# First batch's v rounded in its transfer by GpSimd's queue, the global block last in the first values, w_in issued in two jobs a piece, and a new order of all work

## The chip, the cores and the metric

One core of a Trainium2 chip runs the whole program. The metric is device time in microseconds of that core, the median over several executions. One core has five engines with instruction streams of their own: TensorE (PE in the profile; its weight loads are PEld), VectorE (DVE), ScalarE (ACT), GpSimd (POOL) and SyncE (SP). DMAs are issued from the streams of SP, ACT and GpSimd; all of them are carried out by the same 16 DMA engines.

## The reference

Longformer-like attention over 8 batches, 8 heads, 576 positions of 64 numbers, followed by a two-layer network with softplus between its layers. What is computed:

```
scores = q @ k.T / 8                                       # per batch and head
mask   = |i - j| <= 32, or i global, or j global           # 8 global positions, given as input
attn   = softmax(where(mask, scores, -1e9))
x      = (attn @ v) as 4608 tokens x 512
h      = x @ w_in                                          # 512 x 2048
g      = max(h, 0) + log1p(exp(-|h|))                      # softplus
out    = g @ w_out                                         # 2048 x 512, float32
```

q, k, v, w_in and w_out come as float32 from DRAM; the kernel multiplies in bf16 and accumulates in float32.

## The kernel before

**Blocks.** A batch has 18 blocks of 32 positions. Four blocks make a "pair" n (36 in all), four pairs a tile m of 512 tokens (9 tiles). For one pair, `sc` (L1054) makes the scores of each block against the block before, itself, the block after and the gathered global keys. Then come the maximum `mx`, the exponential `ex` (ScalarE), the sum or its reciprocal `su`, the normalising `no` (GpSimd or VectorE) and a 32x32 transposition `tp` (VectorE). Pairs 0 to 3 are handled in two half-pairs (y = 0 and 1), with the mask added by TensorE itself (`mk`, or within `sc`).

**Global rows.** Queries at global positions see all keys. `add_global` (L948) gives them their own little softmax: scores `sg`, maximum `mxg`, exponential `gexp`, transposition `tpg`, sums of values `ov`, and `gv`, which leaves `vg`, the values that the eight global positions put out and that the values step takes up.

**Values.** `add_values` (L1191) multiplies the normalised weights with v, block by block, into four PSUM banks `xo`, and `xev` copies the banks to `xT`, the transposed tokens. Tile 0 is done in three parts of 128, 256 and 128 tokens (`PIECED`, L357), so that the network can begin early. For each run of blocks the first step of the list (`key` None) is that of the global block, which reads `vg` and opens the accumulation; then come the blocks of keys, which read `vb`.

**Network.** `first` (L1265) makes one chunk of 128 hidden units of h out of `xT` and one quarter of `w_in` (chunks 0 to 3 from piece 0, and so on: the weights come in four pieces of 512 columns, kd 0 and 1 by one DMA, kd 2 and 3 by two). `soft` (L1273) is the softplus on ScalarE, `second` (L1278) the product with `w_out`, `oev` and `store` bring the result out.

**Transfers.** SyncE's queue loads q, k (batches 0 and 1 in six parts each, `load_part`, L512; the order in a batch is `FIRST`) and v (`load_v`, L467: eight DMAs, one for a group of 32 partitions and half the heads, each of 32 x 18 runs of 64 float32) into the float32 tiles `stage`. Engines then round them to bf16 (`cast`, into `qb`, `kb`, `vb`). GpSimd's queue loads `w_in` (`weights_in`, L1331) and `w_out` (`weights_out`) and rounds them on the way. Three holds keep transfers apart: `held` (L1352), a GpSimd copy of one element that waits for the last large q part of batch 0, stands ahead of w_in; `follow` (L753), a tiny DMA on SyncE's queue that reads the end of a weight tile, keeps batch 1's q and k behind w_in's second piece, and batch 1's v behind the first piece of w_out; `landed` (L1416) keeps w_out behind a part of batch 1's k.

**Order.** Each piece of work is a job with its costs and dependencies. `ORDER` (L359) is a written-out list of all jobs: an entry divided by 5 is the job's number in the order of the `add` calls, and the remainder the engine (PE, ACT, DVE, POOL, DMA). So the order within each engine and queue can be read from the list. The jobs' costs in the code are the planner's guesses; the list overrides their choice. Where the planner expects TensorE to be idle in the first 34 us it fills in multiplications of zeros (`warm`, L729).

In the list of before, the queue of GpSimd runs: setup of the mask (`make_near`, `make_neg`, `make_nearer`, `make_keys`), three rounded parts of q and k, `held`, w_in pieces 0 and 1, the two halves of v rounded (`cast` of batch 0, w = 2), w_in piece 2, the normalising of half-pairs 0.1 and 1.0, w_in piece 3, half-pairs 1.1 and 2.1, `make_ends`, `landed`. On SyncE's queue batch 0 comes as q's small part, q part 0, k's three parts, q part 1, v. VectorE makes `gv` of batch 0 behind four maxima of later half-pairs.

## Time and profile before

| | |
|---|---|
| median of three runs | 336.28 us (335.39 to 338.06) |
| the profiled execution, its own time | 334.41 us |
| its span, first to last instruction | 332.7 us |
| TensorE busy | 318.4 us (96%) |
| VectorE, ScalarE, GpSimd busy | 223.6, 225.5, 194.9 us |
| mean granted TensorE clock | 0.995 |

Times in the profile are microseconds from the span's start. In a view in order of time each row has start, length, engine, line, operation, tiles as out<-in, and in brackets how long the engine was idle before and what released it. In a view of groups a row has the count, then the total busy time and the mean of one in ns, then the idle time before. The view of stretches gives, for each stretch, its length, then for PE, PEld, DVE, ACT and POOL the busy time with the number of instructions, then the granted clock, the DMA engines' share and GB/s. A DMA's row stands for its issue; the data arrive later.

### The profile page before, as it was taken

The page shows a single profiled execution, that of the slowest core. Times are in us where ns is not written, and L with a number is a line of the kernel's source. Part 1 is how long each engine was busy: PE and PEld are TensorE (multiplying, and loading weights), DVE is VectorE, ACT ScalarE, POOL GpSimd, SP SyncE. Part 2 cuts the span into 40 slices and gives each one's busy share as a digit, 9 for nine tenths or more (in the row PEclk, how much of TensorE's full clock was granted, in tenths as well). Part 3 has the DMA queues.
Part 4 walks back from the last instruction along what each step waited for, and adds up shares of the span by engine and source line. Part 5 has one row for each costly group of instructions (what it writes and reads, how often), then busy time and mean ns, then how long its engine had stood idle before and what let it go on. Part 6 is the DMA issues. An engine that isn't in the chain of part 4 may idle for free.

```text
span 332.7 us, 12083 instructions
## 1 busy us (share of the span) xinstructions
PE 318.4 (96%) x5279; PEld 170.7 (51%) x5279; DVE 223.6 (67%) x394; ACT 225.5 (68%) x443; POOL 194.9 (59%) x177
## 2 busy tenths in 40 slices
PE   8767799999999999999999999999999999999996
PEld 3536686566555445544454445444544454454453
DVE  6668479977998988897783587839669990440000
ACT  3896577997787669279948963698458547935532
POOL 6496419956795379649979744696274755240000
PEclk9997999999999999999999999999999999999999
DMA  5999999989998999977995996018011011011002
GB/s 155 231 187 205 215 196 163 158 137 237 159 176 135 198 170 168 165 164 154 175 190 137 171 182 111 33 37 205 3 53 46 33 46 77 9 44 53 33 28 98
DMA packets 168860, 42.73 MB, mean 128 GB/s; under 512 B 153320, under 2 KB 165864, under 8 KB 168808
## 3 DMA queue, kind: packets, MB, share of 16 engines
q1 hardware_dynamic: 160664, 28.33, 48.7%
q0 software_dynamic: 6272, 10.49, 13.8%
q10 hardware_dynamic: 1872, 3.15, 2.5%
q8 instruction: 41, 0.67, 0.8%
q14 instruction: 11, 0.09, 0.1%
HBM read 36.71 MB, written 9.44 MB: 139 GB/s over the span
## 4 chain that ended last, share of the span: by engine, by line
PE 88%; DMA 4%; SPq 4%; POOL 2%; issue 1%; ACT 0%
PE o L1281 38%; PE h L1270 37%; PE xo L1235 4%; PE s L1068 3%; DMA win<-in_moe_w_in_dram 3%; SPq L469 2%; DMA stage<-in_v_dram 2%; PE ov L988 2%; PE pick L877 1%; SPq L518 1%; SPq L514 1%; PE sg L959 1%; POOL pn L1123 1%; PE tr L848 1%; POOL win L1335 1%
## 5 line engine op out<-in xcount | busy, mean ns | idle before, releaser
L1270 PE MATMUL h<-xT,win 128*128 128x512 bf16 (+3 forms) x768 | 137.3, 328 | 2.2 <-DMA win<-in_moe_w_in_dram 1.7
L1281 PE MATMUL o<-wout,g 128*128 128x512 bf16 (+1 forms) x592 | 137.0, 374 | 0.0
L1276 ACT ACTIVATE g<-h 128x512 bf16<-128x512 f32 (+3 forms) x192 | 83.9, 499 | 43.4 <-PE h L1270 42.0
L1270 PEld LDWEIGHTS <-win 128*128 128x128 bf16 x768 | 67.5, 99 | 61.2 <-issue 2.7
L1123 POOL TENSOR_TENSOR pn<-st,rs 128x1024 bf16<-128x1024 f32 (+1 forms) x36 | 64.8, 1809 | 40.4 <-DVE rs L1117 28.9
L1281 PEld LDWEIGHTS <-g 128*128 128x128 bf16 x592 | 55.6, 98 | 61.1 <-issue 0.5
L1091 POOL TENSOR_TENSOR st<-st,m 128x1024 f32<-128x1024 f32 x32 | 60.4, 1897 | 30.1 <-DVE m L1085 30.0
L1115 DVE TENSOR_REDUCE sm<-st 128x8 f32<-128x1024 f32 x32 | 38.5, 1203 | 17.2 <-ACT st L1108 17.0
L1072 DVE TENSOR_TENSOR st<-s,mask 128x512 f32<-128x512 f32 x64 | 41.1, 675 | 9.2 <-PE s L1068 9.2
L1085 DVE TENSOR_REDUCE m<-st 128x8 f32<-128x1024 f32 x32 | 38.2, 1205 | 0.4
L1108 ACT ACTIVATE st<-st 128x1024 f32<-128x1024 f32 x32 | 33.0, 1053 | 0.6 <-POOL st L1091 0.5
L1132 DVE STREAM_TRANSPOSE pt<-pn 128x512 int32<-128x512 int32 x36 | 24.6, 690 | 7.8 <-POOL pn L1123 7.6
L720 ACT COPY osb<-o 128x512 f32<-128x512 f32 (+1 forms) x25 | 14.2, 570 | 19.2 <-PE o L1281 17.7
L720 ACT CAST xT<-xo 128x512 bf16<-128x512 f32 (+3 forms) x25 | 11.0, 490 | 16.6 <-PE xo L1235 15.8
L720 DVE CAST xT<-xo 128x512 bf16<-128x512 f32 (+3 forms) x23 | 11.6, 543 | 11.9 <-PE xo L1235 11.9
L1276 ACT ACT_TABLE_LOAD x13 | 16.7, 1283 | 2.6 <-PE h L1270 2.0
L720 POOL CAST vb<-stage 128x1152 bf16<-128x1152 f32 x13 | 15.0, 1167 | 3.9 <-DMA stage<-in_v_dram 3.9
L717 POOL TENSOR_SCALAR qb<-stage 128x1152 bf16<-128x1152 f32 (+2 forms) x12 | 13.3, 1115 | 6.8 <-DMA stage<-in_q_dram 6.8
L1293 POOL DMA_DIRECT2D out_dram<-osb x24 | 13.7, 573 | 5.5 <-DVE osb L720 5.5
L1068 PE MATMUL s<-kx,qx 64*32 64x128 bf16 x1152 | 14.7, 220 | 2.0 <-DVE qx L720 1.5
L1068 PEld LDWEIGHTS <-qx 64*32 64x32 bf16 x1152 | 10.3, 90 | 10.8 <-issue 7.6
L1108 ACT ACT_TABLE_LOAD x12 | 15.4, 1283 | 0.2
(125 smaller groups left out, 293.3 us busy)
## 6 DMA issues: line engine op xcount, KB each, us to landing
stage<-in_v_dram SPq DMA_DIRECT2D x64, 144.0 KB, 4.3
stage<-in_k_dram SPq DMA_DIRECT2D x48, 144.0 KB, 4.1
stage<-in_q_dram SPq DMA_DIRECT2D x48, 144.0 KB, 3.8
out_dram<-osb POOLq DMA_DIRECT2D x24, 256.0 KB, 3.0
out_dram<-osb ACTq DMA_DIRECT2D x11, 256.0 KB, 2.0
stage<-in_q_dram SPq DMA_DIRECT2D x4, 512.0 KB, 7.9
stage<-in_k_dram SPq DMA_DIRECT2D x4, 512.0 KB, 6.9
wout<-in_moe_w_out_dram POOLq DMA_DIRECT2D x4, 512.0 KB, 8.1
```

Source lines behind the costliest of these rows:

```text
L720: {"ACT": nc.scalar.copy, "DVE": V.tensor_copy, "POOL": nc.gpsimd.tensor_copy}[e](out, in_)
L1068: nc.tensor.matmul(out=PS["s", n, g][quad(a), x, :], lhsT=qx[b % 2][rows(g), a, j * BL:(j + 1) * BL], rhs=kx[b % 2][rows(g), a, e0 * BL:(e ...
L1072: V.tensor_tensor(out=PS["st", n][:, h, :, :], in0=PS["s", n, h][:, :, :], in1=mask[:, h, j0:j0 + PB, :, :].rearrange("p j s i -> p j (s i ...
L1085: V.reduce_max(out=m[:], in_=flat(PS["st", n], h0, h1), axis=AX)
L1091: on(e).tensor_tensor(out=t, in0=t, in1=over(PS["m", n, y][:], SL * BL), op=OP.subtract)
L1108: nc.scalar.activation(out=t, in_=t, func=AF.Exp)
L1115: V.reduce_sum(out=sm[:], in_=flat(PS["st", n], h0, h1), axis=AX)
L1123: on(e).tensor_tensor(out=PS["pn", n][:, :, :, h0:h1].rearrange("p x s h -> p h x s"), in0=PS["st", n][:, h0:h1], in1=PS["rs", n, y][:].re ...
L1132: V.transpose(out=bass.AP(base.tensor, base.offset, ap=[list(base.ap[0]), [2 * STEP, PB // 2], [STEP + BL // 2, 2], [1, SL * BL]]), in_=PS ...
L1270: nc.tensor.matmul(out=h[:, :], lhsT=w_in_t[c // 4][:, kd, c % 4 * P:(c % 4 + 1) * P], rhs=PS["xT", m][:, kd, lo:hi], start=(kd == 0), sto ...
L1276: nc.scalar.activation(out=PS["g", m, c][:, lo:hi], in_=PS[key][:, lo_of(c, hi - lo)], func=AF.Softplus)
L1281: nc.tensor.matmul(out=PS["o", m, ns, a][:, :], lhsT=PS["g", m, kf][:, ns * P:(ns + 1) * P], rhs=w_out_t[kf // 4][:, kf % 4, a:z], start=( ...
```

## The change

1. v of batch 0 is no longer loaded by SyncE into `stage` and rounded by GpSimd. GpSimd's queue loads it in four jobs of two DMAs each straight into `vb[0]`, rounding on the way; there is no `cast` for it.
2. `weights_in` is split in two jobs a piece (the DMA of kd 0 and 1; the two of kd 2 and 3), which the order may place apart.
3. Batch 1's q and k wait for w_in's third piece instead of its second (`follow(0, w_in_t[2])`).
4. In the first values (tile 0, first 128 tokens) the global block's step goes from first to last, as a piece of its own that waits for `gv`. As the accumulation must now be opened otherwise, four multiplications by zeros of 128 columns open the four banks.
5. `make_near` and `make_nearer` may run on VectorE; the planner's start of transfers goes from 3050 to 3450.
6. `ORDER` is new throughout. At the start the queue of GpSimd now runs: `make_neg`, one half of q part 0 rounded, the four v jobs, `held`, w_in 0 (both jobs), 1 (both), 2 first job, `make_ends`, 2 second job, 3 first job, half-pair 1.0 normalised, 3 second job, half-pairs 2.0, 2.1, 3.1, a rounded part of batch 1's q, `blank`, another, `landed`. SyncE's has q part 0, k's three parts, q part 1, q's small part, and then batch 1. VectorE takes `make_near`, `make_nearer`, `make_keys` and half-pairs 0.0, 0.1, 1.1 and 3.0. ScalarE runs: four slots of the mask, eight rounded parts of batch 0's q and k with four copies of k between them, then `ex` 0.0, 0.1, a copy of q, `ex` 1.1, a small copy, `ex` 1.0, `gexp` twice, `ex` 2.0, 2.1, `gv`, `ex` 3.1, three copies to `xT`, `ex` 3.0, the first softplus. TensorE has twelve chunks of `first` for the first 128 tokens ahead of the second values (eleven before), four behind them, and then the next 256 tokens' chunks, with batch 1's transpositions behind the first of these (two groups of four stood ahead of them before).

```diff
     def load_v(eng, b, h, rs):
         for c in rs:
-            eng.dma_start(out=stage[2][quad(c), h, :, :],
+            eng.dma_start(out=stage[2][quad(c), h, :, :] if b else vb[0][quad(c), :, h * D:(h + 1) * D],
                           in_=SRC[2][b, HG * h + c].rearrange("(m i) d -> i m d", i=BL))
...
-        if w == 2:
+        if w == 2 and not b:
+            last = None
+            T["cast", 0, 2] = []
+            for h in range(2):
+                for x in range(2):
+                    last = T["half", 0, h] = o.add({"POOL": (1300, 0)}, lambda e, h=h, x=x: load_v(nc.gpsimd, 0, h, range(2 * x, 2 * x + 2)), [last], rank=0,
+                                                   moves=1400, late=1600 if h else 300)
+                    T["cast", 0, 2].append(last)
+            T["load", 0, 2] = last
+        elif w == 2:
...
-                    follow(0, w_in_t[1])
+                    follow(0, w_in_t[2])
...
+        ahead = v_ == 0
+        if ahead:
+            steps = steps[1:] + steps[:1]
...
                 for r in range(KD):
                     PS["xo", v_, r] = psum(("xo", v_, r), [P, 512], FP32)
+                    if ahead:
+                        nc.tensor.matmul(out=PS["xo", v_, r][:, 0:cols], lhsT=idle[:, 0, :], rhs=idle[:, 0, 0:cols], start=True, stop=False)
...
-            ready += [T["gv", b]] + T["cast", b, 2]
+            ready += ([] if ahead else [T["gv", b]]) + T["cast", b, 2]
...
-    def weights_in(x):
+    def weights_in(x, y):
         cols = moe_w_in[:, x * WC:(x + 1) * WC]
-        nc.gpsimd.dma_start(out=w_in_t[x][:, 0:KD // 2, :], in_=cols[0:HD // 2].rearrange("(a p) f -> p a f", p=P))
+        if not y:
+            nc.gpsimd.dma_start(out=w_in_t[x][:, 0:KD // 2, :], in_=cols[0:HD // 2].rearrange("(a p) f -> p a f", p=P))
+            return
...
     for x in range(4):
-        last = T["w_in", x] = o.add({"POOL": (1400, 0)}, lambda e, x=x: weights_in(x), [last or T["held"]],
-                                    rank=-1 if x else 0, hold=2000 if x else 0, moves=2950)
+        for y in range(2):
+            last = T["w_in", x] = o.add({"POOL": (1300 if y else 650, 0)}, lambda e, x=x, y=y: weights_in(x, y), [last or T["held"]],
+                                        rank=-1 if x else 0, hold=2000 if x else 0, moves=1475)
...
-    add_cast(0, 2)
```

More of the change, by code (lines that the diff above doesn't have):

```diff
@@ L106 @@
     DEEP, QUANTUM, RING = 8500, 500, 2600
-    BEGIN = 3050
+    BEGIN = 3450
     PACKETS = {1: 1024, 2: 256, 4: 576, 8: 1152}
```

17 lines of the change are left out of this document (9 added, 8 removed), and 144 rows, old and new, of the table ORDER.

## The prediction

> **What bounds the kernel now.** I read the page first: which engine is full, and which queues move the data.
>
> ```profile
> PE 318.4 (96%) x5279; PEld 170.7 (51%) x5279; DVE 223.6 (67%) x394; ACT 225.5 (68%) x443; POOL 194.9 (59%) x177
> ...
> q1 hardware_dynamic: 160664, 28.33, 48.7%
> q0 software_dynamic: 6272, 10.49, 13.8%
> ```
>
> TensorE is the bound, and its work is not changed but for four multiplications. So only its 14.3 us of idle time (332.7 - 318.4), its filling with zeros and the time at a lower clock can be won. Next, where that lies: the view of TensorE's waits, over the whole execution and after 47 us.
>
> ```profile
> PE xo L1235 <- DVE vg L1001: 2.1, 1, 2.1
> PE h L1270 <- DMA win<-in_moe_w_in_dram: 1.7, 1, 1.7
> PE ov L988 <- POOL vb L720: 1.7, 1, 1.7
> ```
> ```profile
> PE xo L1235 <- issue: 0.4, 1, 0.4
> ```
>
> After 47 us one wait of 0.4 us is left (and the end, which the change leaves as it is). The case is decided by when TensorE enters the stretch without waits. TensorE in order of time, from the first product with w_in on:
>
> ```profile
> 29.03 3.53 PE L1270 MATMUL h<-xT,win 128*128 128x128 bf16 x44
> 32.49 0.32 PE L1235 MATMUL xo<-pt,vg 32*64 32x256 bf16 x8
> 32.63 0.84 PE L1235 MATMUL xo<-pt,vb 32*64 32x32 bf16 x80
> 33.40 0.40 PE L1270 MATMUL h<-xT,win 128*128 128x128 bf16 x4
> 34.32 0.29 PE L1270 MATMUL h<-xT,win 128*128 128x128 bf16 x2 [0.52 <-ACT g L1276]
> 36.33 0.72 PE L1270 MATMUL h<-xT,win 128*128 128x128 bf16 x10 [1.72 <-DMA win<-in_moe_w_in_dram]
> 36.88 0.81 PE L729 MATMUL warm<-vb 128*128 128x512 bf16 x3
> 37.53 0.39 PE L848 MATMUL tr<-ident,kb 128*128 128x128 bf16 x4
> ...
> 38.41 0.81 PE L1270 MATMUL h<-xT,win 128*128 128x256 bf16 x6
> ```
>
> Eleven chunks of the first 128 tokens, the second values at 32.49, then chunks 11 and 12 and a stop: chunk 12 gets two of its four multiplications at 34.32, the others at 36.33, when the late DMAs of w_in's last piece have landed. At 38.41 the chunks of the next 256 tokens begin, and from there TensorE is fed. This 38.41 is the mark that I move. Why was w_in late? GpSimd's and SyncE's queues, and GpSimd's groups of 12 to 29 us:
>
> ```profile
> 14.82 0.95 POOL L1333 DMA_DIRECT2D win<-in_moe_w_in_dram  x1
> ...
> 20.79 1.34 POOL L720 CAST vb<-stage 128x1152 bf16<-128x1152 f32 x1 [0.72 <-DMA stage<-in_v_dram]
> ...
> 26.75 1.21 POOL L1335 DMA_DIRECT2D win<-in_moe_w_in_dram  x2
> ```
> ```profile
> 7.51 0.60 SPq L514 DMA_DIRECT2D stage<-in_q_dram  x1
> 8.16 7.41 SPq L469 DMA_DIRECT2D stage<-in_v_dram  x8
> 24.88 0.73 SPq L757 DMA_DIRECT2D trail<-win  x1
> ```
> ```profile
> L1335 POOL DMA_DIRECT2D win<-in_moe_w_in_dram x8 | 4.9, 627 | 0.0
> L1123 POOL TENSOR_TENSOR pn<-st,rs 128x512 bf16<-128x512 f32 x4 | 4.2, 1079 | 0.0
> L1333 POOL DMA_DIRECT2D win<-in_moe_w_in_dram x4 | 3.2, 805 | 0.0
> L720 POOL CAST vb<-stage 128x1152 bf16<-128x1152 f32 x2 | 2.6, 1283 | 0.7 <-DMA stage<-in_v_dram 0.7
> ```
>
> GpSimd issues w_in from 14.82 to 27.96 (26.75 + 1.21), and 8.1 us of that (4.9 + 3.2) is issuing; the rest is v's rounding (2.6, and 0.7 of waiting for v) and half-pairs. The transfer rates by stretch (5 to 9 us: q and k; 13 to 18: v; 19 to 24: w_in; 27.5 to 31: w_in's end beside batch 1):
>
> ```profile
> 5.00:9.00 4.00, 4.00 (x14) 1.44 (x12) 1.74 (x6) 1.90 (x5) 3.25 (x9) 1.00 1.18 310
> 13.00:18.00 5.00, 4.86 (x119) 2.53 (x114) 3.88 (x13) 4.42 (x17) 4.52 (x8) 1.00 1.39 186
> 19.00:24.00 5.00, 2.23 (x122) 1.61 (x130) 4.04 (x12) 5.00 (x28) 4.28 (x5) 1.00 1.23 197
> 27.50:31.00 3.50, 3.42 (x69) 2.83 (x70) 2.74 (x4) 3.15 (x16) 3.07 (x4) 0.51 1.03 234
> ```
>
> The DMA engines are full all the while; and in the last stretch the granted clock is 0.51, just after the wait for vg.
>
> **The change, part by part.** *v by GpSimd's queue.* What goes: 7.4 us of SyncE's queue (nothing waits behind it until 24.88, so this alone is worth nothing), 2.6 us of rounding on GpSimd, and the wait of `ov` for it (1.7). What comes: eight issues on GpSimd, each of 32 x 18 = 576 runs. No row has so many; the nearest are 627 ns (128 runs) and 805 ns (256), so 5.0 to 6.4 us, and I take the upper end, because the time grows with the runs. They stand behind one rounded half of q part 0, whose arrival ScalarE saw at 7.10:
>
> ```profile
> 7.10 0.63 ACT L713 ACTIVATE qb<-stage 128x512 bf16<-128x512 f32 x1 [5.01 <-DMA stage<-in_q_dram]
> ...
> 16.18 0.39 ACT L1104 ACTIVATE st<-s,m 128x128 f32<-128x128 f32 x1
> ```
>
> That part is now the first on its queue, so 7.10 + 0.6 is a late bound for v's start. v is issued by 7.7 + 6.4 = 14.1 at the latest, 12.7 at the earliest; and `held` costs no wait, as its part, last of the large ones at 7.51 before, has landed by then.
>
> How long v takes to arrive: 4608 runs. At the mean of the hardware queue's packets (48.7% x 332.7 x 16 / 160664 = 16 ns) that is 4.6 us on 16 engines, at the mean of the software queue's (13.8% x 332.7 x 16 / 6272 = 117 ns) 34 us. The nearest row is the same v in the stretch 13 to 18: 1.18 MB at 186 GB/s, 6.3 us. The 117 ns belongs to packets of 1.7 KB (10.49 MB / 6272). I take 6.3, so v is there at about 16 to 17; TensorE's `ov` needs it after 22. So v has some 5 us of slack. The Trainium skill ("DMA: Bandwidth & Descriptors", Specifications) says that transfers under 512 B make the DMA engine read, modify and write, which speaks against this edit, since rounding halves v's written runs from 256 to 128 B. The rows bear it out as far as they go: 186 GB/s for v's 256 B against 310 for q and k; one more such step (x 0.6) would be an estimate of 10.5 us instead of 6.3, still inside the slack, though w_in behind it on the same queue would come up to 4 us later.
>
> *w_in in two jobs.* It starts at about 13.7 instead of 14.82. To the end of piece 3's first job GpSimd has 8.1 - 1.25 = 6.8 us of issuing and one short copy: 21 us. Then half-pair 1.0 (1.08) stands ahead of the last job and waits for VectorE, which gives its factor after the global transposition: about 24 to 25, as below. So the last job is issued at about 25 to 26.2 (27.96 before). Batch 1's q and k now wait for piece 2 and so start later, at about 27; w_in's last 256 KB find the engines empty. Their data alone are 1.3 us at 197 GB/s, which would be 27.5; the 9.6 us from 26.75 to 36.33 once more would be 35.8. With the engines empty I take 31. Batch 1's parts start 1 to 2 us later, but no longer beside 0.5 MB of w_in; their third is due at 35, its transposition on TensorE after 36: margin 1 us, and that is what is late next.
>
> *The way to the second values.* ScalarE's chain starts at 16.18. ScalarE has now more copies ahead of it, VectorE waits for q part 1 instead of GpSimd, six small mask operations go from GpSimd to VectorE (which is busy 1.74 of 4 us between 5 and 9, so they hide). I take 15.5, between 14.8 (q arrives 1.4 us earlier, all else follows) and 16.9. The groups of ScalarE, 13 to 32 us:
>
> ```profile
> L1104 ACT ACTIVATE st<-s,m 128x128 f32<-128x128 f32 x32 | 11.3, 440 | 1.0 <-DVE m L1083 1.0
> ...
> L971 ACT ACTIVATE pg<-sg,gnb 128x320 bf16<-128x320 f32 (+1 forms) x2 | 1.1, 636 | 0.0
> ```
>
> A half-pair is 11.3 / 8 = 1.41. To the first `xT`: seven half-pairs 9.9, one copy and a small one about 1.0 (an estimate from the 0.63 of the same size at 7.10), the global ones 1.1, `gv` 0.3 (an estimate, half of that 0.63), so 27.8, and the copies 0.6: first product at 28.4 (29.03 before). The global block last hides 40 of 48 multiplications of the first values beside `ov` and `gv`; but `gv` is queued on ScalarE behind six half-pairs, so this gains what the wait of 2.1 was only in part: it is in the 28.4. Twelve chunks are 48 multiplications: 44 took 3.53 us with the clock at half for most of it, so 3.9 for 48 at that pace, 2.9 at the 10 in 0.72 less overlap. That gives 31.3 to 32.3; the second values' other inputs (VectorE's half-pair 1.1 behind `ex` 3.1, and two transpositions) come at 30 to 31.8. I take 31.6 for the mark 32.49: 0.9 us won, with 0.25 us of a chunk more done by then.
>
> *The stop.* From the end of the second values (33.47) to 38.41 are 4.94 us. Of these 1.2 are five chunks (20 multiplications at 60 ns), 0.75 two groups of transpositions that now come later. The rest, 3.0, is the waits of 0.52 and 1.72, 0.65 of zeros (36.88 to 37.53) and small change. With w_in landed at 31 all of it goes.
>
> Sum: -0.9 - 0.25 - 3.0, and +0.2 for four opening multiplications: **-3.9 us** at the mark, kept to the end since no wait lies behind it. Against the profiled execution's own 334.41 (span 332.7 and 1.7 around it) that is 330.5. The median of the runs stands 1.9 above the profiled one; from it, 336.28 - 3.9 = **332.4**.
>
> **Rivals.** *1. v delays q and k; no change that can be measured.* The loads of batch 0 were alone on the DMA engines until v followed them on the same queue. Now v comes from another queue while q part 1 is under way. For it: 27.5 to 31, where w_in and batch 1 share the engines and w_in's last DMA needs until 36.33. Against it: from 5 to 9 alone, at 310 GB/s, 1.2 of q and k's 2.4 MB are through, and v begins at 8 or later. Price: if v takes half the packets, q part 1 comes up to 2 to 3 us later, ScalarE's start goes to 18, the front loses 2 to 2.5 and the stop still gains 3.0: -0.5, 335.8. Half of that delay: 334.5. The Trainium skill ("DMA: Bandwidth & Descriptors", Queues, rings and completion order) has each engine go round its queue rows packet by packet, which is this rival's mechanism; that stretch agrees, but no row has two such streams of small runs.
>
> *2. Small packets of the software queue are dear; slower.* w_in stands behind v on one queue. At 117 ns v would end at 42; at 70 ns its 4608 runs take 20 us and end at 29, the first piece of w_in lands at 32 instead of before 29.03, the third chunk (which needs piece 2) waits to 37, and the mark goes to some 41 to 42: 340. It decides from about 50 ns a packet (14.4 us, v at 23, w_in's last piece at 34 to 36). For it: the only mean of that queue is 117. Against: its packets are seven times larger.
>
> *3. More is won.* If the clock stays up over the first chunks (0.51 in 27.5 to 31: 44 multiplications in 3.53 could be 2.6, and the zeros before them) and ScalarE starts at 14.8, another 1.5 to 2: 330.5.
>
> **How the numbers follow.** Forecast, within 1.5 us of 332.4: 0.45; rival 3: 0.13; rival 1 and its half: 0.25; rival 2: 0.17, of which 0.02 small. The range leaves out rival 2's worse part above 338.5, and the tail of rival 3 below 328.5. Runs of this kernel spread by 0.8%, so about 1% (3.4 us, 332.9) is what tells a change from none. Faster: rival 3 and some three quarters of the forecast, 0.48; within 1%: rival 1, the rest of the forecast and rival 2 where small, 0.37; slower: rival 2, 0.15.
>
> **What would show it.** In the changed profile: v's issues on GpSimd at 7 to 14 and of 0.6 to 0.8 us each; first exponential at 15 to 16; no wait of TensorE for v or w_in; the second values near 31.6 and the 256-token chunks near 33.7. If the exponentials start after 17, rival 1 is on; if TensorE waits for w_in longer than 2 us, rival 2. A new wait of TensorE for a part of batch 1 or for w_out would mean that the gain was given back there.

## The result, and the profile after

The changed kernel takes 333.76 us in the median of 12 runs (332.56 to 338.17) against 336.44 us (335.39 to 342.76) of the kernel before beside it: a ratio of 0.9928, 95% interval 0.9907 to 0.9948. That is 0.7% faster, so "within 1%"; 332.4 had been forecast. The profiled execution takes 333.06 us, span 331.4. Now and then an execution is over 1.5% slower than the fastest of its kernel; the ratios, and the counts of runs by clock under "The median and the profiled run", leave these out.

The page of the changed kernel, the rows that answer to those of before:

```profile
PE 317.9 (96%) x5281; PEld 168.8 (51%) x5281; DVE 220.9 (67%) x387; ACT 231.7 (70%) x460; POOL 193.3 (58%) x173
...
q1 hardware_dynamic: 155928, 27.15, 46.0%
q0 software_dynamic: 11008, 11.08, 17.0%
```

The queue of GpSimd (q0) has 4736 packets more: v's 4608 and 128 others. TensorE is as full as before. Now GpSimd and ScalarE at the start, in order of time (start, length, engine, line, operation, tiles):

```profile
6.20 5.53 POOL L469 DMA_DIRECT2D vb<-in_v_dram  x8
...
12.86 0.73 POOL L1350 DMA_DIRECT2D win<-in_moe_w_in_dram  x1 [0.42 <-DMA vb<-in_v_dram]
...
24.45 1.24 POOL L1353 DMA_DIRECT2D win<-in_moe_w_in_dram  x2
```
```profile
14.96 0.35 ACT L1113 ACTIVATE st<-s,m 128x128 f32<-128x128 f32 x1
```

v is issued from 6.20 to 11.73, w_in from 12.86 to 25.69 (14.82 to 27.96 before), and the exponentials begin at 14.96 (16.18). TensorE, from the global rows' values to the chunks of 256 tokens:

```profile
22.81 1.23 PE L997 MATMUL ov<-vb,pgt 32*32 32x129 bf16 x72 [0.99 <-DVE pgt L987]
...
25.06 0.64 PE L1237 MATMUL xo<-vb 128*128 128x128 bf16 x4
25.69 0.49 PE L1251 MATMUL xo<-pt,vb 32*64 32x64 bf16 x40
25.99 0.29 PE L1251 MATMUL xo<-pt,vg 32*64 32x128 bf16 x8
...
27.63 2.84 PE L1286 MATMUL h<-xT,win 128*128 128x128 bf16 x48 [0.81 <-DMA win<-in_moe_w_in_dram]
30.40 0.32 PE L1251 MATMUL xo<-pt,vg 32*64 32x256 bf16 x8
...
31.38 1.94 PE L1286 MATMUL h<-xT,win 128*128 128x128 bf16 x24
```

The last row joins multiplications that follow without a gap and names the shape of the first: the last 16 for the first 128 tokens, then eight for the next 256. A view from 32.5 us on shows the eight in a row of their own:

```profile
32.28 1.04 PE L1286 MATMUL h<-xT,win 128*128 128x256 bf16 x8
```

The wait for the rounded v and the stop for w_in are gone. The mark, the first chunk of 256 tokens, came from 38.41 to 32.28: 6.1 us. Of these 0.7 are two groups of transpositions that stood ahead of the mark before and now stand behind it (33.15 and 34.79), so TensorE is 5.5 us ahead with the same work. But the last store is issued only 1.8 us earlier (330.07 before, 328.25 after), and the span is 1.3 us shorter. The view of stretches shows where the rest went; here are the kernel before and then the changed one (length, busy time of each engine with its number of instructions, granted clock, transfer share, GB/s):

```profile
38.00:46.00 8.00, 7.69 (x177) 6.79 (x176) 3.87 (x7) 6.57 (x22) 4.88 (x12) 1.00 0.99 159
46.00:54.00 8.00, 7.92 (x212) 7.02 (x212) 6.94 (x12) 3.99 (x15) 4.28 (x4) 1.00 0.96 181
54.00:62.00 8.00, 8.00 (x90) 4.15 (x89) 7.86 (x14) 7.79 (x13) 7.65 (x5) 1.00 1.24 181
62.00:70.00 8.00, 8.00 (x183) 4.58 (x181) 7.74 (x18) 7.41 (x16) 7.66 (x6) 1.00 0.83 131
```
```profile
38.00:46.00 8.00, 7.62 (x222) 5.94 (x220) 6.99 (x11) 6.64 (x22) 2.83 (x4) 1.00 1.11 168
46.00:54.00 8.00, 6.41 (x153) 4.05 (x151) 5.80 (x9) 4.73 (x16) 6.67 (x5) 1.00 1.22 193
54.00:62.00 8.00, 8.00 (x115) 4.16 (x114) 7.16 (x13) 5.02 (x8) 4.69 (x4) 1.00 1.03 167
62.00:70.00 8.00, 6.90 (x182) 4.58 (x180) 5.89 (x11) 7.54 (x17) 7.74 (x6) 1.00 0.90 143
```

TensorE (first busy column) works 31.6 of 32 us in the kernel before and 28.9 in the changed one: of the gain 2.7 us are lost as idle time between 38 and 70 us, 1.5 of them in 46 to 54 and 1.1 in 62 to 70. (The 5.5 us are 1.7 at 69 us, so 3.8 are given back; of the other 1.1 these columns show nothing.) In order of time, the rows of the changed kernel there:

```profile
47.16 0.68 PE L1077 MATMUL s<-kx,qx 64*32 64x128 bf16 x56 [0.58 <-issue]
52.81 0.43 PE L968 MATMUL sg<-kx,qg 128*32 128x320 bf16 x8 [1.00 <-issue]
57.77 1.14 POOL L720 CAST vb<-stage 128x1152 bf16<-128x1152 f32 x1 [3.31 <-DVE sm L1124]
60.80 1.06 ACT L1117 ACTIVATE st<-st 128x1024 f32<-128x1024 f32 x1 [2.96 <-POOL st L1100]
64.67 0.22 PE L1251 MATMUL xo<-pt,vg 32*64 32x64 bf16 x4 [0.40 <-ACT osb L720]
66.60 1.90 POOL L1132 TENSOR_TENSOR pn<-st,rs 128x1024 bf16<-128x1024 f32 x1 [0.26 <-DMA stage<-in_q_dram]
69.31 0.38 PE L1251 MATMUL xo<-pt,vg 32*64 32x384 bf16 x8 [0.23 <-DVE pt L1141]
```

Two things are to be seen. TensorE stands twice with nothing to wait for but its own instructions ("issue", 0.58 and 1.00). And GpSimd stands 3.31 us ahead of a rounding (57.77), which is the second half of batch 1's v; behind it on GpSimd is a subtraction for the softmax, for which ScalarE stands 2.96 us, and because ScalarE is late with its copies out of PSUM, TensorE stands at the values between 63.9 and 65.3 (0.40 us at 64.67, for a copy on ScalarE). The last of four products on GpSimd ends at 68.50, and 0.81 us later, after a transposition on VectorE, TensorE begins the values that need it (32x384, "the fifth values" below).

### The profile page after: what moved, and what is told of

Same layout as the page of the kernel before. It is cut to its first block, busy times and chain, and to the rows that moved or that the text cites. A ratio compares the mean times of both kernels' runs of the same rounds, so it can differ in the third digit from the quotient of the medians.

```text
span 331.4 us, 12080 instructions
## 1 busy us (share of the span) xinstructions
PE 317.9 (96%) x5281; PEld 168.8 (51%) x5281; DVE 220.9 (67%) x387; ACT 231.7 (70%) x460; POOL 193.3 (58%) x173
## 4 chain that ended last, share of the span: by engine, by line
PE 71%; SPq 11%; DMA 9%; ACT 4%; issue 1%; POOL 1%; DVE 1%; POOLq 0%
PE o L1297 32%; PE h L1286 29%; SPq L464 5%; PE xo L1251 4%; DMA stage<-in_q_dram 4%; SPq L469 3%; PE s L1077 3%; DMA stage<-in_k_dram 3%; ACT st L1113 2%; DMA wout<-in_moe_w_out_dram 2%; PE ov L997 1%; DMA stage<-in_v_dram 1%; SPq L518 1%; PE pick L886 1%; SPq L514 1%
## 5 line engine op out<-in xcount | busy, mean ns | idle before, releaser
L1297 PE MATMUL o<-wout,g 128*128 128x512 bf16 (+1 forms) x592 | 138.6, 374 | 0.2 <-ACT g L1292 0.2
L1286 PEld LDWEIGHTS <-win 128*128 128x128 bf16 x768 | 66.7, 98 | 59.7 <-issue 1.1
L720 ACT COPY osb<-o 128x512 f32<-128x512 f32 (+1 forms) x27 | 15.5, 575 | 20.3 <-PE o L1297 18.7
L720 POOL CAST kb<-stage 128x1152 bf16<-128x1152 f32 (+2 forms) x9 | 11.5, 1273 | 10.8 <-DMA stage<-in_q_dram 8.8
L717 POOL TENSOR_SCALAR qb<-stage 128x1152 bf16<-128x1152 f32 (+1 forms) x11 | 12.9, 1177 | 8.1 <-DMA stage<-in_q_dram 6.5
L720 POOL CAST vb<-stage 128x1152 bf16<-128x1152 f32 x9 | 10.3, 1150 | 6.8 <-DVE sm L1124 3.3
```

Source lines behind the costliest of these rows:

```text
L720: {"ACT": nc.scalar.copy, "DVE": V.tensor_copy, "POOL": nc.gpsimd.tensor_copy}[e](out, in_)
L1286: nc.tensor.matmul(out=h[:, :], lhsT=w_in_t[c // 4][:, kd, c % 4 * P:(c % 4 + 1) * P], rhs=PS["xT", m][:, kd, lo:hi], start=(kd == 0), sto ...
L1297: nc.tensor.matmul(out=PS["o", m, ns, a][:, :], lhsT=PS["g", m, kf][:, ns * P:(ns + 1) * P], rhs=w_out_t[kf // 4][:, kf % 4, a:z], start=( ...
```

## The experiments

My first theory was that both kinds of stop had given the gain back and that each could be taken away by itself. The rival was that ScalarE and GpSimd are full behind 50 us and take back any lead. (In `ORDER` the cuts show the entries that move; the lines they stand in are broken anew, and no other entry changes its place.)

**The changed kernel once more,** as the yardstick of the next three.

> The changed kernel itself, as the yardstick for the three kernels that run beside it: both theories expect the ratio measured first, 0.991 to 0.995 of the kernel before.

332.88 us, ratio 0.9918 (0.9884 to 0.9951). Its rows, for the comparisons:

```profile
57.55 1.14 POOL L720 CAST vb<-stage 128x1152 bf16<-128x1152 f32 x1 [2.32 <-DMA stage<-in_v_dram]
66.37 1.90 POOL L1132 TENSOR_TENSOR pn<-st,rs 128x1024 bf16<-128x1024 f32 x1 [0.26 <-DMA stage<-in_q_dram]
69.07 0.38 PE L1251 MATMUL xo<-pt,vg 32*64 32x384 bf16 x8 [0.22 <-DVE pt L1141]
```

Here the rounding's wait is put down to what it reads, the transfer of v. (VectorE's sum, named in the first trace, is no input of it.)

**Batch 1's v rounded behind the subtraction.** Entry 2008 (the rounding on GpSimd) goes behind 1923 (the subtraction of pair 7):

```diff
     ORDER = (
...
-        2008,
...
         1923,
+        2008,
```

> One step moved: GpSimd rounds the second half of batch 1's v behind the fourth subtraction, not ahead of it. In the changed kernel GpSimd stood 3.31 us ahead of that rounding (54.46 to 57.77), ScalarE then 2.96 us for the subtraction behind it (57.84 to 60.80), and TensorE some 1.5 us at 63.5 to 65.3, where the banks of the fourth values were freed late. My theory: what was won ahead of 38 us was given back at single places of the order, this one among them, so the subtraction starts near 54.5, ScalarE's wait falls below 1 us, TensorE's stop at the fourth values falls from about 1.5 us to under 0.4, and the time by 0.8 to 1.5 us against the changed kernel (ratio to the kernel before near 0.989 to 0.990). The rival: from 50 us on ScalarE and GpSimd are full and take back whatever TensorE is ahead, so the stop moves to a later place and the time stays within 0.4 us of the changed kernel.

331.89 us, ratio 0.9866 (0.9816 to 0.9917; the interval overlaps that of the changed kernel beside it). The trace:

```profile
56.99 1.90 POOL L1100 TENSOR_TENSOR st<-st,m 128x1024 f32<-128x1024 f32 x1 [2.05 <-DVE m L1094]
58.83 1.14 POOL L720 CAST vb<-stage 128x1152 bf16<-128x1152 f32 x1
59.94 7.46 POOL L1132 TENSOR_TENSOR pn<-st,rs 128x1024 bf16<-128x1024 f32 x4
...
64.33 0.24 PE L1251 MATMUL xo<-pt,vg 32*64 32x64 bf16 x8
...
68.20 0.38 PE L1251 MATMUL xo<-pt,vg 32*64 32x384 bf16 x8
```

The stop at the fourth values (64.33) is gone, the four products end at 67.40 and the fifth values come at 68.20, 0.87 us earlier than in the kernel beside it; the span is 0.9 us shorter (330.2 for 331.1). That is the lower end of the expected 0.8 to 1.5. ScalarE's wait fell as expected, to 0.60 us, but the subtraction came at 56.99 and not near 54.5, because it now waited 2.05 us for a maximum on VectorE instead.

**TensorE's stops for instructions.** Ten second products are spread ahead of the dense scores (1945, 1855: pairs 8 and 6; 2010: the global block), and two softplus steps on ScalarE (1181, 1176) come forward with them:

```diff
+        1420, 1585, 1590, 1595, 1600, 1181, 1176,
         1945, 1855,
...
+        1620, 1495, 1500, 1505, 1425,
         2010,
```

(The same entries are taken out further on.)

> Five second products are moved ahead of the scores of pairs 8 and 6, and five ahead of the global block's scores of batch 1 (two softplus steps are moved forward on ScalarE to free their bank). In the changed kernel TensorE stood 0.58 us inside the first scores and 1.00 us ahead of the second with nothing to wait for but its instructions, each time until 1.35 us behind the end of a 16-KB transfer of instructions. My theory: these are the instruction fetch, 64 matmuls and as many weight loads in 0.7 us use up what is loaded; with second products there, which use 2 instructions in 0.22 us, both stops shrink to under 0.3 us each and the time falls by 0.5 to 1.5 us against the changed kernel. The rival: the fetches are asked for by the instructions issued, so they come later by as much, and the stops move to the next dense place: time within 0.4 us.

334.98 us, ratio 0.9981 (0.9943 to 1.0018); the profiled run has 332.58 and span 330.9.

```profile
69.03 0.38 PE L1251 MATMUL xo<-pt,vg 32*64 32x384 bf16 x8 [0.23 <-DVE pt L1141]
```

Both stops for instructions are gone from the trace, and nothing came of it: the fifth values start at 69.03 (69.07). So the stops were real, but not on the path; this half of my theory fell. TensorE only arrived earlier at a place where it waits for GpSimd. Why the median lies 2.1 us over the changed kernel's while the trace is as fast, the traces don't show: 6 of its 12 runs were granted a clock of 0.995 or less, but so were 5 of the 12 of the changed kernel beside it. That stays open.

**Both together.**

> Both moves together. My theory: they lie at different places of the same chain of TensorE's work and add, 1.3 to 3.0 us less than the changed kernel, which gives a ratio to the kernel before of 0.984 to 0.989. The rival (a full ScalarE or GpSimd behind 50 us takes it back): no more than 0.5 us less than the changed kernel.

332.94 us, ratio 0.9911 (0.9877 to 0.9946); fifth values at 69.08, span 331.1: no gain, as the rival said. The scores of pair 8 now come later, VectorE and then GpSimd start later by as much, and the rounding comes so late (59.71) that TensorE stands 1.29 us ahead of the product that reads it. What the spread products put off was the start of GpSimd's chain.

**The parts of the change, one by one.** First, the order of the blocks in the first values, undone:

```diff
-        ahead = v_ == 0
+        ahead = False
...
-        at = [p * len(steps) // pieces for p in range(pieces + 1)] if not ahead else [0, len(steps) - 1, len(steps)]
+        at = [p * len(steps) // pieces for p in range(pieces + 1)] if v_ else [0, len(steps) - 1, len(steps)]
```

> The changed kernel with the global block first in the first values again, so that all of them wait for the global values; the opening multiplications by zeros (four, 0.64 us) fall away. My theory: the global values are ready within 0.3 us of the first values' start in the changed kernel (keys' values from 25.69, global ones at 25.99), so this part of the change is worth next to nothing: time within 0.4 us of the changed kernel, either side. The rival: the order of the blocks is worth the 0.5 us and more that the kernel before waited there, 0.5 to 1 us slower than the changed kernel.

334.13 us, ratio 0.9929 (0.9901 to 0.9957), not to be told from the changed kernel.

```profile
25.73 0.47 PE L1251 MATMUL xo<-pt,vg 32*64 32x128 bf16 x8 [0.52 <-ACT vg L1008]
```

The first values wait 0.52 us for the global ones, and the second values come at 30.38, as with the change (30.40). By the times this part is worth nothing here. Its profiled run took 335.65 us: TensorE stood 1.44 and 1.87 us for instructions (until 32.24 and 45.45), at other places than in the changed kernel, from which this one differs by eight instructions ahead of there; and from 46.62 to 50.03 the granted clock was 0.50. So here the fifth values come at 71.61, 2.3 us later than in the changed kernel.

Then the last piece of w_in, its two jobs together again:

```diff
-        98, 103, 425, 296,
+        98, 103, 108, 425, 296,
```

> The changed kernel with the two jobs of the fourth piece of w_in one behind the other on GpSimd, ahead of the product it used to stand between. My theory: the product's inputs come at 23.46 anyway, 2.42 us after the first job's issue, so 1.24 us of issue fit in between, the fourth piece lands about 3 us earlier, and the time is the same within 0.4 us, as the piece wasn't waited for. The rival: the split is where the gain comes from, the product is late and the time 0.5 us or more above the changed kernel.

333.54 us, ratio 0.9927 (0.9897 to 0.9957): the split of this piece is worth nothing either. The trace shows something else:

```profile
49.87 0.68 PE L1077 MATMUL s<-kx,qx 64*32 64x128 bf16 x56 [1.80 <-issue]
...
61.18 0.80 PE L997 MATMUL ov<-vb,pgt 32*32 32x129 bf16 x72
```
```profile
69.31 0.38 PE L1251 MATMUL xo<-pt,vg 32*64 32x384 bf16 x8
```

TensorE is 1.9 us behind the changed kernel at 61.18 (59.24 in the repeat), after 1.80 us of waiting for instructions, and yet the fifth values start only 0.24 us later. Up to there TensorE has that much slack; GpSimd has none.

And the hold on batch 1's parts, back to w_in's second piece:

```diff
-                    follow(0, w_in_t[2])
+                    follow(0, w_in_t[1])
...
-            T["part", b, w, t] = o.add({"DMA": (700 if b else 0, 0)}, emit, had(("w_in", 2)) + T["cast", 0, w] if b else [], rank=0,
+            T["part", b, w, t] = o.add({"DMA": (700 if b else 0, 0)}, emit, had(("w_in", 1)) + T["cast", 0, w] if b else [], rank=0,
```

> The changed kernel with batch 1's parts held only for the second piece of w_in, as before, not for the third: their transfers run beside the last two pieces. My theory: the parts start 2 to 4 us earlier, the copy of batch 1's keys that the scores waited 0.4 us for at 40 us is earlier, and the third and fourth pieces land later; the first products would wait for w_in some 1 us or more, as the transfers share the 16 engines: time 0 to 1 us above the changed kernel. The rival: the hold costs more than it gives, the earlier parts take 0.4 us or more off the time.

333.92 us, ratio 0.9949 (0.9920 to 0.9979).

```profile
31.78 0.27 PE L1286 MATMUL h<-xT,win 128*128 128x128 bf16 x2 [1.59 <-DMA win<-in_moe_w_in_dram]
```

The stop for w_in is back, 1.59 us (1.72 in the kernel before), as expected; the second values come 1.6 us later. So it is the hold that removes that stop. But the fifth values come at 69.22, 0.15 us later, and the time isn't to be told from the changed kernel's. The rival, that earlier parts are worth more, falls.

**GpSimd's chain made earlier.** With these results I formed the theory anew: behind 50 us the path is the maxima on VectorE, the subtractions on GpSimd, the rounding of batch 1's v when it has landed, four products, a transposition, the fifth values. So the step that the subtraction waited for in the run of the later rounding was moved: VectorE takes the maximum of the global block's scores (2017) behind that of pair 7 (1917).

```diff
-        2008,
...
         1923,
+        2008,
...
-        2017,
...
         1917,
+        2017,
```

> The later rounding again (GpSimd rounds the second half of batch 1's v behind the fourth subtraction), and on VectorE the maximum of the global block's scores of batch 1 behind the masks and the maximum of pair 7 instead of ahead of them. With the later rounding alone the subtraction still stood 2.05 us for that maximum (54.95 to 56.99) and the rounding was over at 59.97, too late for the global values' product, which waited. My theory: the maximum then comes near 55, the subtraction starts within 0.4 us of 54.95, the rounding within 0.5 us of v's landing near 57.5; TensorE's wait ahead of the global values' product goes, no stop at the fourth values, the fifth values start 1.5 to 2.5 us earlier than the 69.07 of the changed kernel, and all behind that by as much: time 1.3 to 2.5 us under the changed kernel (ratio 0.983 to 0.988). The rival: GpSimd's products behind it (7.46 us for four) or ScalarE hold the fifth values where they were with the later rounding alone (68.20): at most 1 us under the changed kernel.

332.67 us in 6 runs, ratio 0.9905 (0.9868 to 0.9942); the profiled run 331.6, span 329.9.

```profile
56.30 1.90 POOL L1100 TENSOR_TENSOR st<-st,m 128x1024 f32<-128x1024 f32 x1 [0.61 <-DVE m L1094]
58.14 1.14 POOL L720 CAST vb<-stage 128x1152 bf16<-128x1152 f32 x1
59.25 7.47 POOL L1132 TENSOR_TENSOR pn<-st,rs 128x1024 bf16<-128x1024 f32 x4
...
67.83 0.38 PE L1251 MATMUL xo<-pt,vg 32*64 32x384 bf16 x8
```

The products end at 66.72, 1.55 us earlier than in the changed kernel's repeat, the fifth values start 1.24 us earlier, and the span is 1.2 us shorter (329.9 for 331.1). By the trace the direction held, but the size stayed under the expected 1.3 to 2.5 us: the scores ahead of the chain stood 1.33 us for instructions in this run, and the subtraction before this one came at 51.95, 0.75 us later than with the later rounding alone (51.20). By the times the rival came ("at most 1 us under"): 332.67 against 332.88 us, and the interval of the ratio overlaps that of the changed kernel.

**And with the second products spread.**

> As the kernel before this one, and the ten second products moved ahead of the scores of pairs 8 and 6 and of the global block's scores, so that the instruction fetch is not waited for. My theory: TensorE's two stops of 0.55 and 0.9 us go as well, and since the rounding no longer stands in the way of the products, they are kept: 0.3 to 1 us under the kernel beside it, 2 to 3 us under the changed kernel. The rival: the fifth values are set by GpSimd's chain (subtraction, rounding at v's landing, four products), which TensorE's earlier hand-over does not move: the fifth values start within 0.3 us of the kernel beside it and the times agree within 0.4 us.

331.82 us in 6 runs, ratio 0.9887 (0.9851 to 0.9922); fifth values at 68.10, span 330.2. By the time it is as the theory said, 0.85 us under the kernel before it, though the intervals overlap; by the trace it is as the rival said, with the fifth values 0.27 us later and the span 0.3 longer. The stops for instructions are gone, but the later scores cost GpSimd 0.6 us (products from 59.82), so the theory's way to its number isn't what the trace shows.

Over these ten traces, all with the changed kernel's front or nearly so, the fifth values start 0.80 to 1.11 us after GpSimd's last product ends, wherever that is, and the span ends 261.8 to 262.3 us behind them (last product's end, fifth values, span):

```
changed kernel                 68.50   69.31   331.4
changed kernel, repeat         68.27   69.07   331.1
spread                         68.23   69.03   330.9
spread, later rounding         68.28   69.08   331.1
global block first             70.62   71.61   333.9
w_in's last together           68.32   69.31   331.4
hold on second piece           68.23   69.22   331.5
later rounding                 67.40   68.20   330.2
later rounding, maximum        66.72   67.83   329.9
both, and spread               67.30   68.10   330.2
```

In six of them TensorE stands for the transposition behind the last product and starts 0.05 us after it ends. In the other four (global block first, w_in's last together, the hold, the maximum) it starts 0.24 to 0.36 us after it, so there TensorE itself is the later one, by that little.

**The first part alone.** Batch 0's v by GpSimd's queue in the kernel before, with the old order otherwise: four issues in GpSimd's idle time from 8.6 us, four ahead of w_in.

```diff
     ORDER = (
...
+        34, 183,
         283,
...
+        39, 188,
         63,
...
-            eng.dma_start(out=stage[2][quad(c), h, :, :],
+            eng.dma_start(out=stage[2][quad(c), h, :, :] if b else vb[0][quad(c), :, h * D:(h + 1) * D],
...
+                if w == 2 and not b:
+                    load_v(nc.gpsimd, b, h, range(R))
```

> The kernel before with one part of the change: batch 1's predecessor, batch 0's v, goes by GpSimd's queue straight to its rounded place, four issues in GpSimd's idle time from 8.6 us (before its first rounding) and four ahead of the first job of w_in; its two roundings on GpSimd fall away; the rest of the order is the old one. My theory: v lies there by about 20.5 us, TensorE's stops of 1.68 us for the rounded v at 20.5 and most of the 2.10 us for the global values at 25.5 go, the start of the 256-token chunks comes 1.5 to 2.5 us earlier than 38.41, and 0.5 to 2 us of the time are won (ratio 0.994 to 0.998): part of the gain, since the exponentials still begin where they did. Rival 1 of the prediction: the small packets take transfer time from q and k, so the second q part is rounded over 0.5 us later than 13.47 and the time stays within 0.5 us of the kernel before. Rival 2: dear packets, slower by over 1 us.

338.35 us, ratio 1.0051 (1.0021 to 1.0081): 0.5% slower. But the run doesn't answer the question, since the planner's costs had put 13 multiplications by zeros into TensorE's way at 13.88 and the first scores came 4.5 us late:

```profile
13.88 3.36 PE L729 MATMUL warm<-vb 128*128 128x512 bf16 x13
```

So once more, with the two costs set so that the zeros stand where they stood in the kernel before:

```diff
-                T["half", b, h] = o.add({"DMA": (2200 if b else 0, 0)}, emit, deps, rank=0, units=R, moves=3100 if b else 2800, late=LATE if b else 1300 * h)
+                T["half", b, h] = o.add({"DMA": (2200 if b else 0, 0)}, emit, deps, rank=0, units=R, moves=3100 if b else 0, late=LATE if b else 1300 * h)
...
-                cost = {"POOL": (1150, 1250), "DVE": (760, 850)}
+                cost = {"POOL": (2000, 5000) if w == 2 else (1150, 1250), "DVE": (760, 850)}
```

> The kernel before with batch 0's v alone sent by GpSimd's queue to its rounded place, as the run of that part before, but without the 13 multiplications by zeros that had been put ahead of the 64-token key transposes there and held the first scores to 18.30 (13.83 in the kernel before). Four issues lie in GpSimd's idle time from 8.6 us, four ahead of the first job of w_in, no roundings. My theory: the first scores come within 0.7 us of 13.83, TensorE's stop of 1.68 us for v at 20.5 goes, w_in's first jobs start 2.9 us later (17.7 for 14.8) but its third at 22 as before; 0 to 2 us of the time are won, less than the changed kernel's 2.7, since the old order still starts the exponentials late. The rival: the new place for v is worth nothing without the new order, since what is late next (the queries' rows at 20.09 and the global values at 27.58) was late by as much: within 0.5 us of the kernel before, either side.

338.17 us, ratio 1.0063 (1.0034 to 1.0093). The first scores came at 14.84, 0.3 us beyond the bound expected, with the clock at 0.50 from 12.48 to 15.90, but the front was then ahead: the third values at 42.77 (44.52 before), the global block's scores of batch 1 at 53.17 (55.23). Then:

```profile
61.15 1.15 ACT L720 CAST vb<-stage 128x1152 bf16<-128x1152 f32 x1 [5.77 <-DMA stage<-in_v_dram]
65.99 0.80 PE L988 MATMUL ov<-vb,pgt 32*32 32x129 bf16 x72 [3.81 <-ACT st L1108]
```

Again it is batch 1's v: ScalarE stands 5.77 us for its second half, TensorE 3.81, and the lead of 2 us becomes a lag (fifth values at 74.94, 70.97 before). The clock has a part in that lag: behind the stop it was 0.50 for 3.41 us (67.10 to 70.51), which costs some 1.7 us (an estimate, half of 3.41). In the kernel before the same rounding started at 57.34 without a wait. What had changed for that transfer? It is issued at 45.62 to 50.99 (45.16 to 51.12 before), but the third and fourth pieces of w_out came on GpSimd's queue at 49.24, 2.3 us earlier than before (51.57), since the subtraction ahead of them came at 47.39 instead of 49.72. So the last run moves the fourth piece of w_out behind the rounding and one subtraction:

```diff
-        823, 1969, 1978, 1808,
+        1969, 1978, 1808, 823,
```

> As the kernel before with batch 0's v alone sent by GpSimd's queue, and the fourth piece of w_out issued behind GpSimd's rounding of batch 1's v and one subtraction (near 54.5 us) instead of ahead of both (50.1). In the run without this edit the early part was ahead of the kernel before by 1.75 us at the third values (42.77 for 44.52) and by 2.06 us at the global block's scores of batch 1 (53.17 for 55.23); then ScalarE stood 5.77 us for the second half of batch 1's v (61.15), TensorE 3.81 us, and the end was 2.2 us later than in the kernel before. My theory: v of batch 1, on SP's queue, shared the transfer engines there with 512 KB that came 2.3 us earlier than in the kernel before; without them ScalarE's rounding starts 1.5 to 3 us before 61.15, TensorE's stop falls to 1 to 2.3 us, the fifth values come 1.5 to 2.6 us before 74.94, and the time is 1.5 to 2.6 us under that run's. The rival: the landing is set by the queue that v stands in, the packets ahead of it and their rate, not by what GpSimd's queue moves: landing within 0.7 us of 61.15 and the time within 0.5 us of that run's.

335.78 us, ratio 1.0008 (0.9973 to 1.0043).

```profile
59.28 1.16 ACT L720 CAST vb<-stage 128x1152 bf16<-128x1152 f32 x1 [3.20 <-DMA stage<-in_v_dram]
64.13 0.80 PE L988 MATMUL ov<-vb,pgt 32*32 32x129 bf16 x72 [1.33 <-ACT st L1108]
```

The landing comes 1.87 us earlier and TensorE's stop falls to 1.33, though the front was 0.7 to 1 us later this time (third values at 43.75, after a clock of 0.50 from 11.72 to 18.55); the fifth values come at 72.37, 2.57 us earlier, and the time falls by 2.4 us: the theory's numbers. The rival, a landing within 0.7 us, falls. 512 KB on GpSimd's queue had held back v on SyncE's. Not all of the 2.4 us is the landing's, as behind this shorter stop the clock doesn't fall to half. And with this mended the first part is still only equal to the kernel before. The Trainium skill ("DMA: Bandwidth & Descriptors", Queues, rings and completion order) has each transfer engine go round the queues that have work; these two runs agree, with 1.87 us as the price here.

## Why the prediction was right, and where it was wrong

333.76 us lies in the range of 328.5 to 338.5, 1.4 us over the forecast. The mechanism was right up to the mark, the size there was too small, and the way from the mark to the end was wrong. Step by step:

- *v by GpSimd's queue.* Start at 6.20 ("7.10 + 0.6 is a late bound"), eight issues in 5.53 us (bounds 5.0 to 6.4, the upper end taken): 0.69 each. In the trace's packet records v's 4608 packets run from 10.5 to 16.1 us, 5.7 us (6.3 taken, there "at about 16 to 17"). That 6.3 was a quotient of bytes and rate; v's 256-byte packets in the kernel before ran from 12.1 to 20.0, 8.0 us. The Trainium skill's rule on transfers under 512 B ("DMA: Bandwidth & Descriptors", Specifications), worked out in the prediction to an estimate of 10.5 us, is not borne out as a further slow-down here: the 128-byte runs took 5.7 us against 8.0 for the 256-byte ones, with a packet at 32 ns against 28 in the median. No engine's computing waited for batch 0's v; GpSimd's issues of w_in stood 0.42 and 0.41 us (12.86 and 15.39), which the trace puts down to v's transfer.
- *w_in in two jobs.* Last issue at 25.69 (25 to 26.2). TensorE's one wait put down to w_in is the 0.81 ahead of the first product. ScalarE's copies to `xT` end at 27.58 and the product starts at 27.63, so it is hardly w_in; in the run with the global block first the same place reads 0.57 for ScalarE's copies. Whether two jobs a piece were needed is another matter: for the last piece they weren't; it is the hold on the third piece that took the stop of 1.72 away.
- *The way to the second values.* Exponentials at 14.96 (15.5), first product at 27.63 (28.4), 48 multiplications in 2.84 us (3.9 to 2.9), second values at 30.40 (31.6). Each is at the good end of its bounds, and 2.1 us are won here instead of 0.9. For the multiplications that is the clock, which was 1.00; why the exponentials came 0.5 us before the forecast is open. These are nearly the conditions of rival 3 (clock up, ScalarE from 14.8).
- *The stop.* Gone; chunks of 256 tokens at 32.28 (33.7). On work done 5.5 us were won instead of 3.9, as rival 3 had it.
- *The margin that "is late next"*, batch 1's third part: TensorE stood 0.38 us at 40.36 for the copy of batch 1's keys. Batch 1's first part was issued at 25.86 (25.73 before), not "1 to 2 us later".
- *"Kept to the end since no wait lies behind it".* This is the step that failed. 5.5 us were won at the mark, 1.7 at the fifth values, 1.8 at the last store. The prediction's own condition for that case, a new wait for a part of batch 1, came true in another form: TensorE doesn't wait for batch 1's v itself, but GpSimd does, in front of a subtraction, and TensorE meets GpSimd's chain at the fourth and fifth values.

So the nearness of the number is partly luck. By the profiled execution 330.5 was forecast and 333.06 measured: 1.35 us won instead of 3.9. The front won 1.6 more than forecast, and 3.8 were given back; and the changed kernel's median stands only 0.7 above its profiled execution, where the forecast carried over 1.9 from the kernel before.

The row that I could have read is in the trace of before, in order of time:

```profile
68.03 1.90 POOL L1123 TENSOR_TENSOR pn<-st,rs 128x1024 bf16<-128x1024 f32 x1 [0.34 <-DMA stage<-in_q_dram]
...
69.97 0.71 DVE L1132 STREAM_TRANSPOSE pt<-pn 128x512 int32<-128x512 int32 x1
...
70.97 0.38 PE L1235 MATMUL xo<-pt,vg 32*64 32x384 bf16 x8
```

No wait is listed there, but the transposition ends at 70.68 and TensorE reads its result at 70.97: a margin of 0.29 us. Whatever TensorE wins ahead of that beyond 0.29 us is kept only as far as GpSimd's chain comes earlier too. The chain came 1.43 us earlier (last product's end 69.93 to 68.50), and the fifth values 1.66: the 1.43 and most of the margin. With that reading the sum would have ended not at TensorE's -3.9 but at what GpSimd's chain wins, which measured as -1.7 with the margin.

*Rivals.* Rival 1 (v delays q and k): no; the exponentials began 1.2 us earlier, not later. Rival 2 (dear packets, "from about 50 ns"): v's packets took 32 ns in the median, 49 in their slowest stretch, and w_in wasn't late. Rival 3 had its clock and its mark, but not its time: what it wins was given back.

*The median and the profiled run.* The profiled runs differ by 1.35 us (334.41 to 333.06), the medians by 2.7. The remainder goes with the granted clock: 85 of 89 runs of the kernel before in these comparisons had less than 0.998 (on average 0.987), and 7 of 22 of the changed kernel (on average 0.998). Grouped by clock, the two are closer: 333.8 and 333.0 us at 0.998 and above (4 and 15 runs), 334.7 and 334.6 at 0.995 (6 and 4). So a part of the measured gain comes with a clock that stays up. Where it falls can be seen in the profile of before, in two stretches of 3.41 us each:

```profile
24.11:27.52 3.41, 1.38 (x36) 0.42 (x9) 2.36 (x6) 2.42 (x15) 3.41 (x5) 1.00 1.02 151
27.52:30.93 3.41, 3.35 (x68) 2.76 (x69) 2.65 (x4) 3.06 (x16) 3.05 (x4) 0.50 1.03 235
```

TensorE is busy for 1.38 us of the first, around its wait for the global values, and gets half the clock in the second. The same pair is seen with the global block first (1.55 of 3.42 us, then 0.50) and with the first part alone (1.11 of 3.41 behind the stop of 3.81, then 0.50). In the changed kernel the emptiest such stretch of the front, 16.39 to 19.80, has 1.92 us of work, and the clock stays at 1.00. That the fuller start keeps the clock up agrees with these traces; no run was made to test it, and not every gap does it: after the 1.80 us at 49.87 with w_in's last jobs together it stayed at 1.00.

What is shown, then: the change brings the front forward by 5.5 us; neither the order of the blocks nor the split of the last piece is needed for the time; the hold on the third piece removes the stop for w_in, and without it the time isn't told from the changed kernel's either; the first part alone, in the old order, wins 0.8 to 2 us in front and loses them behind, in part because a w_out issued earlier holds back batch 1's v; and the end is set, to within 0.4 us, by when GpSimd's chain is through. Rounding batch 1's v behind the subtraction, and the maximum moved, gives 1.2 us more by the trace (span 329.9); by the times it isn't told from the changed kernel.

What isn't shown: how much of the front comes from the new order of all work, and how much from the masks made on VectorE, as no run takes either by itself; and whether w_out (issued at 48.62 in the changed kernel) holds back batch 1's v there too, as it does with the first part alone.

## What to carry to other kernels

A list of waits says who was late, not by how little the others weren't: before a gain is carried to the end, look at the next place where the engine meets another's result and read the margin there. A gain at the start survives only as far as every chain that meets it comes earlier. And work that comes earlier issues its next transfers earlier; ask which transfer on another queue they will stand beside. Read a row that joins several shapes with care: the mark itself was hidden in one here.

## What was not expected of the hardware

- Eight issues of 576 runs each on GpSimd's queue took 0.69 us apiece, between the 0.63 of 128 runs and the 0.81 of 256: the issue time didn't grow with the runs.
- v's 128-byte packets on that queue took 32 ns (median from 10 to 12 us and from 14 to 16) and 49 ns from 12 to 14 us, while 425 packets of the hardware queue (q1) ran too. In the three runs with the first part alone, where v comes in two parts, the last packets of the first part, from 14 us on, took some 80 ns. Why, the traces don't show.
- TensorE's "issue" stops of 0.58 and 1.00 us both ended 1.3 to 1.4 us after a 16-KB transfer on the instruction queue (ends at 45.82 and 51.44, stops over at 47.16 and 52.81); in the kernel before one of 0.39 us ended 1.28 us after such a transfer, and the four longer ones in other runs 1.4 to 1.6 us after. They lie in or behind scores, 32 multiplications and as many weight loads in 0.42 us, and move when a few instructions are added or taken away anywhere ahead (1.80 us at 49.87 in one kernel, none in another). Taken away by themselves they gave nothing; ahead of GpSimd's chain (1.33 us with the maximum moved) one delays it.
